# Softmax weights turned by VectorE's 32x32 block transposes and one trip through DRAM, from the tenth pair of heads on

## The chip, the core and the metric

The kernel runs on one core of one Trainium2 chip. The metric is the device time of one execution in microseconds (us). A core has five engines that run side by side, each through its own list of instructions in order: TensorE (PE in the profile; its weight loads are PEld), VectorE (DVE), ScalarE (ACT), GpSimd (POOL) and SyncE (SP). In this kernel SP issues every DMA; the DMAs run on 16 DMA engines and read or write DRAM.

## The reference

What is computed is windowed attention with a linear position bias, followed by two gated feed-forward blocks. Shapes: 4 sequences of 576 tokens (2304 rows), 8 heads of 64; the first block is 512 to 2048 and back, the second 512 to 1536 and back.

```python
def _attn_ref(q, k, v):
    scores = scale * np.matmul(q, k.transpose(0, 1, 3, 2))
    rel = pos[:, None] - pos[None, :]
    mask = (rel >= 0) & (rel < 128)
    scores = np.where(mask, scores + slopes * (-np.abs(rel)), -1e9)
    attn = softmax(scores)                       # over keys
    return np.matmul(attn, v)

def reference(q, k, v, w_in, w_out, w_gate, w_val, w_out2, rms_g):
    x = heads_side_by_side(_attn_ref(q, k, v))   # 2304 x 512
    h = x @ w_in
    x = (h * np.clip(h + 3, 0, 6) / 6) @ w_out
    xn = x / rms(x) * rms_g
    g = xn @ w_gate
    return (g * sigmoid(g) * (xn @ w_val)) @ w_out2
```

## The kernel before

**Blocks, pairs, steps.** The 2304 tokens are 18 tiles of 128 rows, taken as six blocks of three tiles. Attention works on a pair of heads at a time: four pairs for each block, 24 pairs in all, numbered 0 to 23. A pair has three steps, one for each tile of queries. Each query sees 128 keys, which lie in two neighbouring tiles, so a row of the upper key tile and a row of the lower one never both hold a live weight in the same column. From pair 9 on (`JOINT = 9`, the tenth) a step folds both key tiles into one 128x128 tile per head before the exponential (line 378) and unfolds them after the transpose with two `affine_select`s on POOL (line 407), one that keeps one side of the diagonal and one that keeps the other.

**One step.** `scores` (TensorE) makes queries times keys; `bias` (VectorE, lines 371 and 378) adds the bias; `exp` (ScalarE, line 386) takes the exponential and its sum, and POOL the reciprocal (lines 388 and 389); `divide` (VectorE, line 394) scales the rows. The weights then stand with queries on the partitions, while the product with V needs keys there. `transpose` turns them: one TensorE transpose for each head and live key tile, into PSUM (line 400). `weights` copies the result to an SBUF tile `pt` (ScalarE, line 405) and runs the two selects (POOL, line 407). `values` multiplies with V (TensorE, line 418).

**Slots.** The first feed-forward block runs in 96 slots, 16 for each block of tokens. A slot m holds a product with `w_in` into the PSUM tile `ps_h` (line 484, 12 matmuls), the gate on ScalarE and VectorE (lines 722, 723, 728, 734), which makes `g`, and the product of the slot before with `w_out` (line 497, 9 matmuls), which reads that slot's `g`. The attention of the next block of tokens is laid into the slots. For a pair whose first slot is t0 a table `plan` gives the slots of its parts (`S` scores, `D` divide, `T` and `L` transpose, `V` values), and a loop over the slots issues them at fixed places:

```python
t0, plan = AHEAD + M1 * (b - 1) - 2 + 4 * j, {"S": (0, 0, 0), "D": (1, 1, 2),
    "T": (None, 2, 3), "L": (1, None, None), "V": (5, 5, 5)}
```

Three numbers are the slots, after t0, of a pair's three steps. Pairs start four slots apart, so slots t0+4 and t0+5 of a pair are t0 and t0+1 of the next. `T` puts the transposes behind the slot's product with `w_in`, `L` behind the product with `w_out`. Nothing reorders instructions: each engine works in the order in which the code issues them.

**Other work in the slots.** From the third block on (called part 3 in the code) each slot but those with m % 4 = 2 also prepares a piece of the second block's weights: `W2.turn` converts one 512 KB piece on ScalarE and VectorE (lines 131 to 147), and SP loads a later piece (`load`, line 202) and stores the converted one (lines 224 and 230). There are 36 pieces. `Norm` scales the rows of the first block's result, turns them on TensorE (line 550) and stores them (`store`, line 541, the transfers `x<-yt`) in some of the slots. After the 96 slots comes the second feed-forward block (lines 845, 892), which the change does not touch.

## Time and profile before

| What | us |
|---|---|
| time, median of 3 runs (956.23 to 956.37) | 956.29 |
| span of the profiled execution, first to last instruction | 954.2 |
| TensorE matmuls busy in that span | 937.7 |
| VectorE busy | 640.5 |
| ScalarE busy | 454.2 |
| GpSimd busy | 186.3 |

The span is counted on the chip from the first to the last instruction; the 2.1 us by which the median is longer lie around it. The page gives the profiled execution's time by this span. Pairs 9 to 23 lie between about 140 and 460 us of it. A matmul's end is modelled and overlaps the start of the next, so what a matmul takes of TensorE's time is read from start to start.

### The profile page before, as it was taken

To read this page: it belongs to the slowest core of one execution; us is meant where nothing else is said; L and a number is where in the kernel's file an instruction comes from. 1 tells how busy PE (TensorE), PEld (TensorE's weight loads), DVE (VectorE), ACT (ScalarE), POOL (GpSimd) and SP (SyncE) were. 2 spreads that over 40 slices of the span, in tenths; PEclk is the share of its full clock that TensorE was granted. 3 is DMA by queue.
4 is the path that set the end of the run, shared out by engine and by line. 5 is a ranking of instruction groups with operands and counts; after the bars stand their busy time and mean duration, and the time that the engine had idled before them with its cause. 6 is when DMAs were issued, how large, how long until landed. Compare 5 with 4: busy or idle time off the path is not lost.

```text
span 954.2 us, 14654 instructions
## 1 busy us (share of the span) xinstructions
PE 937.7 (98%) x5336; PEld 832.9 (87%) x5336; DVE 640.5 (67%) x1336; ACT 454.2 (48%) x969; POOL 186.3 (20%) x327
## 2 busy tenths in 40 slices
PE   7899999999999999999999999999999999999998
PEld 4587888888888888888899999999999999999996
DVE  5788667555878777877467657777545577545555
ACT  6899566455666655655455453433131323231120
POOL 4333012332223332422124223310000000000000
PEclk8999999999999999999999999999999999999999
DMA  6555401113666555554355757866757555755521
GB/s 231 183 194 194 187 20 51 32 53 117 198 211 203 172 164 174 164 169 130 122 182 210 287 206 293 320 229 234 249 212 281 214 202 199 265 206 211 214 86 67
DMA packets 67432, 175.02 MB, mean 183 GB/s; under 512 B 5024, under 2 KB 41888, under 8 KB 62624
## 3 DMA queue, kind: packets, MB, share of 16 engines
q1 hardware_dynamic: 67360, 174.09, 52.2%
q8 instruction: 42, 0.69, 0.3%
q14 instruction: 30, 0.25, 0.1%
HBM read 130.03 MB, written 44.04 MB: 182 GB/s over the span
## 4 chain that ended last, share of the span: by engine, by line
PE 87%; DVE 6%; ACT 4%; issue 2%; POOL 1%; ACTq 0%; POOLq 0%; DVEq 0%
PE ps_o L497 19%; PE ps_h L484 18%; PE ps_y L892 15%; PE ps_o L845 10%; PE ps_S L845 8%; PE ps_A L845 6%; PE ps_h L845 4%; PE ps_av L418 2%; PE ps_t L400 2%; PE ps_s L357 1%; DVE wx L143 1%; PE ps_s L348 1%; ACT t L386 1%; ACT wx L136 1%; DVE t L371 1%
## 5 line engine op out<-in xcount | busy, mean ns | idle before, releaser
L497 PE MATMUL ps_o<-w,g 128*128 128x512 f32 x864 | 224.0, 402 | 2.1 <-DVE w L147 1.9
L484 PE MATMUL ps_h<-xs,w 128*128 128x384 f32 x1152 | 220.2, 339 | 0.0
L484 PEld LDWEIGHTS ps_h<-xs,w 128*128 128x128 f32 x1152 | 202.4, 188 | 5.8 <-issue 0.2
L497 PEld LDWEIGHTS ps_o<-w,g 128*128 128x128 f32 x864 | 156.2, 188 | 41.1 <-issue 6.3
L892 PE MATMUL ps_y<-wo,g 128*128 128x512 f32 x648 | 150.2, 390 | 0.5 <-DVE g L881 0.5
L892 PEld LDWEIGHTS ps_y<-wo,g 128*128 128x128 f32 x648 | 121.3, 188 | 25.1 <-DVE g L881 0.9
L723 DVE SCALAR_TENSOR_TENSOR t<-t,ps_h 128x384 f32<-128x384 f32 x96 | 53.2, 554 | 98.7 <-ACT t L722 98.6
L722 ACT ACTIVATE t<-ps_h,three 128x384 f32<-128x384 f32 x96 | 55.5, 578 | 84.1 <-PE ps_h L484 80.2
L899 DVE TENSOR_TENSOR y<-y,ps_y 128x512 f32<-128x512 f32 x90 | 61.7, 686 | 35.3 <-PE ps_y L892 35.0
L386 ACT ACTIVATE t<-t,m 128x128 f32<-128x128 f32 (+1 forms) x144 | 61.4, 428 | 29.4 <-DVE t L378 14.2
L728 ACT CAST g<-t 128x384 fp32r<-128x384 f32 x96 | 49.5, 516 | 47.5 <-DVE t L723 46.2
L734 DVE TENSOR_TENSOR g<-t,g 128x384 fp32r<-128x384 f32 x96 | 54.4, 567 | 23.3 <-ACT g L728 23.0
L868 ACT ACTIVATE r<-r 128x384 f32<-128x384 f32 x36 | 19.0, 527 | 105.6 <-DVE r L867 105.6
L845 PE MATMUL ps_o<-S,tw 128*128 128x384 f32 x336 | 66.2, 339 | 0.3 <-DVE t L865 0.3
L388 POOL TENSOR_SCALAR r<-den 128x2 f32<-128x2 f32 x72 | 27.4, 380 | 187.6 <-ACT t L386 186.0
L845 PEld LDWEIGHTS ps_o<-S,tw 128*128 128x128 f32 x336 | 59.3, 188 | 1.4 <-DVE u L856 0.8
L389 POOL TENSOR_TENSOR r<-r,minus 128x2 f32<-128x2 f32 x72 | 56.0, 778 | 6.0
L407 POOL TENSOR_SCALAR_AFFINE_SELECT pt<-pt 128x256 f32<-128x256 f32 x82 | 34.5, 421 | 107.5 <-ACT pt L405 104.5
L853 ACT COPY s<-ps_S 128x384 f32<-128x384 f32 x18 | 8.7, 481 | 86.9 <-PE ps_S L845 86.9
L371 DVE CUSTOM_DVE_ANT_0 t<-ps_s,rel 128x256 f32<-128x256 f32 (+2 forms) x128 | 45.2, 395 | 3.6 <-PE ps_s L357 3.6
L143 DVE SCALAR_TENSOR_TENSOR wx<-wx,wy 128x512 uint32<-128x512 uint32 (+1 forms) x52 | 44.2, 850 | 0.0
L136 ACT ACTIVATE wx<-wraw 128x512 f32<-128x512 f32 (+1 forms) x52 | 42.8, 824 | 0.0
(138 smaller groups left out, 1471.9 us busy)
## 6 DMA issues: line engine op xcount, KB each, us to landing
tw<-t SPq DMA_DIRECT2D x52, 896.0 KB, 6.3
wraw<-w SPq DMA_DIRECT2D x36, 512.0 KB, 4.1
wo<-w SPq DMA_DIRECT2D x18, 1024.0 KB, 4.9
wraw<-w SPq DMA_DIRECT2D x16, 1024.0 KB, 9.1
t<-th SPq DMA_DIRECT2D x12, 896.0 KB, 4.3
t<-tl SPq DMA_DIRECT2D x12, 896.0 KB, 4.3
b<-wx SPq DMA_DIRECT2D x24, 256.0 KB, 2.6
w<-w SPq DMA_DIRECT2D x12, 512.0 KB, 3.0
```

The source lines that it names most:

```text
L143: vec.scalar_tensor_tensor(out=xi, in0=xi, scalar=3, in1=y, op0=ALU.logical_shift_left, op1=ALU.bitwise_or)
L371: vec.tensor_tensor_reduce(out=self.t[:, a, c0:], in0=s[:, c0:], in1=(rel_split if self.i in SPLITS else rel)[:, c0:], scale=2.0 ** (-8.0 ...
L386: act.activation(p, p, AF.Exp, bias=self.m[:, a : a + 1], scale=-1.0, accum_out=self.den[:, a : a + 1])
L389: pool.tensor_tensor(self.r, self.r, minus, ALU.pow)
L484: pe.matmul(ps[:, : n * P], lhsT=w[:, a, c * P : (c + 1) * P], rhs=xs[c][:, b, : n * P], start=(k == 0), stop=(k == 3 * KC - 1),)
L497: pe.matmul(o, lhsT=g[:, a, i * P : (i + 1) * P], rhs=w[:, b], start=(m == first and a == 0 and b == 0), stop=(m == last and a == 1),)
L722: act.activation(r[:, :nq], ps[:, :nq], AF.Relu, bias=three)
L723: vec.scalar_tensor_tensor(out=r[:, :nq], in0=r[:, :nq], scalar=6.0, in1=ps[:, :nq], op0=ALU.min, op1=ALU.mult)
L734: vec.tensor_sub(g[:, 1, :nq], r[:, :nq], f32(g[:, 0, :nq]))
L845: pe.matmul(ps, lhsT=w[a][:, k, c * P : (c + 1) * P], rhs=x[:, b, c], start=(start and j == 0), stop=(j == 5), skip_group_check=True,)
L892: pe.matmul(ps, lhsT=gs[i + k][:, a, t // 3, t % 3 * P : (t % 3 + 1) * P], rhs=wo[i + k][:, b], start=(k == 0 and a == 0 and b == 0), stop ...
L899: vec.tensor_add(acc[t], acc[t], ps)
```

## The change

From pair 9 on a step's weights are no longer turned by TensorE. `turn` lets VectorE transpose the 32x32 blocks of each head's folded 128x128 tile in place of the grid (block row and block column stay where they are), from the upper half of the tile `t` into its lower half, and SP stores that half to a DRAM tile `pd` (128 KB, rows of 512 bytes). When a pair's three steps are stored, `fetch` reads them back with four DMAs, one for each group of 32 partitions, which put block (b, a) where block (a, b) was: 96 KB each, in runs of 32 elements (128 bytes). The result is the turned tile, in `pt`. The copy by ScalarE is gone, and the two selects on POOL stand in a method of their own. `pt` is one fixed tile with a place for each of the three steps, and its two middle dimensions are exchanged. In the slots, divide and values keep their places; `turn` stands in the slots of the divide, behind the low half of `g`; `fetch` (`R`) at the start of slot t0+3; the selects (`W`) of all three steps at the start of slot t0+4. Pairs 0 to 8 keep TensorE's transposes.

A second edit: the load of a later piece in `W2` moves from `turn` to the end of `begin`, so that it stands behind the first three conversion steps of the piece whose buffer it takes, and a piece is loaded one turn earlier than before.

```diff
@@ Second.begin and Second.turn
                 for _ in range(3):
                     next(self.run)
+                self.load()
...
             x = run.send(None)
-            self.load()
             if kind < 2:
                 self.begin()
                 sp.dma_start(out=self.whole[m][:, kind::2], in_=x.rearrange("p (a k) -> p a k", a=2))
@@ Pair
+        def fetch(self):
+            for k in range(0, P, 32):
+                sp.dma_start(
+                    out=weights_[k : k + 32, 1].rearrange("r u a (b s) -> r (u a b) s", s=32),
+                    in_=self.d[:, :, :, k : k + 32].rearrange("u a (b r) s -> r (u a b) s", r=32),
+                )
@@ Step
+            self.via = self.joint or self.c0 == P and pair.b * H // 2 + pair.j >= JOINT
+            self.pt = weights_[:, :, u]
...
+        def turn(self):
+            t, pr = self.t[:, :, :P], self.pair
+            if self.first:
+                pr.d = dram.tile([3, 2, P, P], F32, tag="pd", name="pd", bufs=2)
+            vec.transpose(t, self.t[:, :, P:])
+            sp.dma_start(out=pr.d[self.u].rearrange("a p k -> p a k"), in_=t)
...
         def weights(self):
-            self.pt = ap.tile([P, 2, 2, P], F32, tag="pt", name="pt", bufs=3)
-            act.copy(self.pt[:, :, self.p0 // P :], self.ps[:, :, self.p0 // P :])
+            act.copy(self.pt[:, self.p0 // P :], self.ps[:, self.p0 // P :])
+            self.select()
+
+        def select(self):
             for c, sign in ((0, -1), (1, 1)) if self.joint else ():
@@ the plan of a pair's steps
-            for kind, at in plan.items():
+            steps = {"S": plan["S"], "D": plan["D"], "R": (None, None, 3), "W": (4, 4, 4), "V": plan["V"]} if step.via else plan
+            for kind, at in steps.items():
@@ the loop over the slots
             late = l_
+            for x in r_:
+                x.pair.fetch()
+            for x in w_:
+                x.select()
             ps = ps_h.tile([P, 4 * P], F32, tag="h", name="ps_h")
...
             vec.tensor_sub(g[:, 1, :nq], r[:, :nq], f32(g[:, 0, :nq]))
+            for x in d_:
+                if x.via:
+                    x.turn()
```

Three places show what the order of instructions becomes. On TensorE, the five products after the values of pair 20 (`ps_av`), in which pair 21's three steps were turned (`ps_t`); `ps_h` and `ps_o` are the two products of a slot. Line 484 becomes 506, 497 becomes 519, 418 becomes 439.

```order
L418 MATMUL ps_av<-pt,vraw 64x128 x12
L497 MATMUL ps_o<-w,g 128x512 x9
L400 MATMUL ps_t<-ident,t 128x128 x2
L484 MATMUL ps_h<-xs,w 128x384 x12
L400 MATMUL ps_t<-ident,t 128x128 x2
L497 MATMUL ps_o<-w,g 128x512 x9
L484 MATMUL ps_h<-xs,w 128x384 x12
L400 MATMUL ps_t<-ident,t 128x128 x2
L497 MATMUL ps_o<-w,g 128x512 x9
```

```order
L439 MATMUL ps_av<-pt,vraw 64x128 x12
L519 MATMUL ps_o<-w,g 128x512 x9
L506 MATMUL ps_h<-xs,w 128x384 x12
L519 MATMUL ps_o<-w,g 128x512 x9
L506 MATMUL ps_h<-xs,w 128x384 x12
L519 MATMUL ps_o<-w,g 128x512 x9
```

The three groups of two transposes are gone, and nothing takes their place on TensorE.

On SP, slots t0+1 to t0+3 of pair 21 (`wraw` is the load of a piece of weights, `b` and `w` its converted store, `x<-yt` the store of a normed tile, `pd` and `pt` the new trip):

```order
L297 DMA vraw<-v 128x4x128
L202 DMA wraw<-w 128x512
L230 DMA w_4_133<-w 128x1024
L202 DMA wraw<-w 128x512
L224 DMA b_114<-wx 256x1x256
L541 DMA x_1_139<-yt 512x1x128
L202 DMA wraw<-w 128x512
L224 DMA b_114<-wx 256x1x256
```

```order
L298 DMA vraw<-v 128x4x128
L413 DMA pd<-t 128x2x128 x2
L202 DMA wraw<-w 128x512
L230 DMA w_4_133<-w 128x1024
L413 DMA pd<-t 128x2x128
L202 DMA wraw<-w 128x512
L224 DMA b_114<-wx 256x1x256
L563 DMA x_1_140<-yt 512x1x128
L323 DMA pt<-pd 32x24x32 x4
L202 DMA wraw<-w 128x512
L224 DMA b_114<-wx 256x1x256
```

The last of the three stores and the four reads stand with a load, a store of weights and a store of `x` between them.

On VectorE, slots t0+1 and t0+2 of a pair, after: the transposes stand behind the low half of `g` (line 760) and ahead of the scaling of the norm and the conversion of weights. Before, the same rows stood there without line 412.

```order
L760 TENSOR_TENSOR g<-t,g 128x384
L412 STREAM_TRANSPOSE t<-t 128x2x128 x2
L556 TENSOR_SCALAR y<-y,ri 128x512
L143 SCALAR_TENSOR_TENSOR wx<-wx,wy 128x512
L133 TENSOR_SCALAR wy<-wraw 128x512
L140 TENSOR_SCALAR wy<-wraw 128x512
L147 TENSOR_TENSOR w<-wx,w 128x512
L749 SCALAR_TENSOR_TENSOR t<-t,ps_h 128x384
L405 TENSOR_SCALAR t<-t,r 128x128 x2
L760 TENSOR_TENSOR g<-t,g 128x384
L412 STREAM_TRANSPOSE t<-t 128x2x128
```

Two steps of the pair are turned in slot t0+1 and the third in slot t0+2, where its divide (line 405, 394 before) is.

## Rows read from the trace of the kernel before

**Rows 1.** The page: span, and busy us with shares of the engines.

```profile
span 954.2 us, 14654 instructions
...
PE 937.7 (98%) x5336; PEld 832.9 (87%) x5336; DVE 640.5 (67%) x1336; ACT 454.2 (48%) x969; POOL 186.3 (20%) x327
```

**Rows 2.** Busy us (and instructions) by stretch: PE, PEld, DVE, ACT, POOL; clock, DMA share, GB/s.

```profile
300.00:400.00 100.00, 100.00 (x654) 87.90 (x653) 77.95 (x212) 61.15 (x161) 31.96 (x67) 1.00 0.53 168
```

**Rows 3.** Timeline of PE around pair 23: start us, us, what, count.

```profile
441.27 2.34 PE L497 MATMUL ps_o<-w,g 128*128 128x512 f32 x9
443.45 0.38 PE L400 MATMUL ps_t<-ident,t 128*128 128x128 f32 x2
443.58 2.34 PE L484 MATMUL ps_h<-xs,w 128*128 128x384 f32 x12
...
452.44 2.27 PE L484 MATMUL ps_h<-xs,w 128*128 128x384 f32 x12
...
460.29 2.33 PE L497 MATMUL ps_o<-w,g 128*128 128x512 f32 x9
462.46 2.27 PE L484 MATMUL ps_h<-xs,w 128*128 128x384 f32 x12
464.57 2.24 PE L497 MATMUL ps_o<-w,g 128*128 128x512 f32 x9
466.65 0.69 PE L484 MATMUL ps_h<-xs,w 128*128 128x384 f32 x3
```

**Rows 4.** Groups by line, 140 to 460 us: busy us, mean ns, idle before.

```profile
L407 POOL TENSOR_SCALAR_AFFINE_SELECT pt<-pt 128x256 f32<-128x256 f32 x82 | 34.5, 421 | 107.5 <-ACT pt L405 104.5
...
L400 PE MATMUL ps_t<-ident,t 128*128 128x128 f32 x90 | 17.4, 274 | 0.3 <-ACT pt L405 0.2
...
L405 ACT COPY pt<-ps_t 128x256 f32<-128x256 f32 x45 | 16.5, 366 | 3.9 <-PE ps_t L400 3.8
L378 DVE TENSOR_TENSOR t<-t 128x256 f32<-128x256 f32 x37 | 15.7, 425 | 1.3
```

**Rows 5.** Timeline of DVE, slot t0+2 of pair 21.

```profile
403.85 0.56 DVE L723 SCALAR_TENSOR_TENSOR t<-t,ps_h 128x384 f32<-128x384 f32 x1 [0.71 <-ACT t L722]
...
404.99 0.56 DVE L734 TENSOR_TENSOR g<-t,g 128x384 fp32r<-128x384 f32 x1 [0.16 <-ACT g L728]
...
407.04 0.46 DVE L140 TENSOR_SCALAR wy<-wraw 128x512 uint16<-128x512 uint16 x1
```

**Rows 6.** The page's DMA issues: count, KB each, median us to landing.

```profile
x<-yt SPq DMA_DIRECT2D x18, 256.0 KB, 3.0
```

**Rows 7.** Timeline of SP, pair 21: start and us of each issue.

```profile
407.19 0.57 SPq L541 DMA_DIRECT2D x<-yt  x1
407.87 0.58 SPq L202 DMA_DIRECT2D wraw<-w  x1
```

**Rows 8.** Timeline of SP, 143 to 150 us, where few transfers run.

```profile
149.01 0.38 SPq L297 DMA_DIRECT2D vraw<-v  x1
```

**Rows 9.** Stretches of 1 us, columns as in Rows 2: DMA share and GB/s.

```profile
112.00:113.00 1.00, 1.00 (x8) 1.00 (x7) 0.00 (x0) 0.00 (x0) 0.00 (x0) 1.00 1.00 426
144.00:145.00 1.00, 1.00 (x6) 0.81 (x5) 0.97 (x5) 0.89 (x4) 0.00 (x0) 1.00 0.77 199
145.00:146.00 1.00, 1.00 (x7) 0.95 (x6) 1.00 (x5) 0.77 (x4) 0.86 (x2) 1.00 0.72 260
...
150.00:151.00 1.00, 1.00 (x6) 0.83 (x5) 1.00 (x3) 1.00 (x2) 0.00 (x0) 1.00 0.49 144
151.00:152.00 1.00, 1.00 (x9) 0.92 (x6) 1.00 (x2) 1.00 (x2) 0.00 (x0) 1.00 0.42 126
```

**Rows 10.** Timeline of PE: the values of pair 21, slot t0+5.

```profile
418.18 1.53 PE L418 MATMUL ps_av<-pt,vraw 128*64 128x128 f32 x24
```

**Rows 11.** Timeline of POOL, slot t0+4 of pair 21: the next pair's reciprocals.

```profile
415.98 0.22 POOL L388 TENSOR_SCALAR r<-den 128x2 f32<-128x2 f32 x1 [5.92 <-ACT t L386]
416.28 0.87 POOL L389 TENSOR_TENSOR r<-r,minus 128x2 f32<-128x2 f32 x1
```

More of the change, by code (lines that the diff above doesn't have):

```diff
@@ L62 @@
 PAIRS2 = NTILE // 6
-KINDS = "QSDTLV"
+KINDS = "QSDTLVRW"
 OPEN = {"reuse_waits": "tile"}
@@ L274, in fused_kernel @@
     xs_of = {}
+    weights_ = ap.tile([P, 2, 3, 2, P], F32, tag="pt", name="pt", bufs=1)
     class Pair:
@@ L399, in transpose @@
                 for c in range(self.p0 // P, 2):
-                    pe.transpose(self.ps[:, a, c], self.t[:, a, c * P : (c + 1) * P], ident)
+                    pe.transpose(self.ps[:, c, a], self.t[:, a, c * P : (c + 1) * P], ident)
         def weights(self):
-            self.pt = ap.tile([P, 2, 2, P], F32, tag="pt", name="pt", bufs=3)
-            act.copy(self.pt[:, :, self.p0 // P :], self.ps[:, :, self.p0 // P :])
+            act.copy(self.pt[:, self.p0 // P :], self.ps[:, self.p0 // P :])
+            self.select()
+        def select(self):
             for c, sign in ((0, -1), (1, 1)) if self.joint else ():
                 pool.affine_select(
-                    out=self.pt[:, :, c], in_=self.pt[:, :, 1], compare_op=ALU.is_ge, fill=0.0,
+                    out=self.pt[:, c], in_=self.pt[:, 1], compare_op=ALU.is_ge, fill=0.0,
                     base=c - 1, pattern=[[0, 2], [sign, P]], channel_multiplier=-sign,
@@ L420, in values @@
                         lhsT=pr.vr[:, self.i - 1 + c - pr.lo, a * D : (a + 1) * D],
-                        rhs=self.pt[:, a, c],
+                        rhs=self.pt[:, c, a],
                         start=(c == self.from_),
@@ L577, in fused_kernel @@
     for t in range(AHEAD):
-        q, s_, d_, t_, _, v_ = at(t)
+        q, s_, d_, t_, _, v_, _, _ = at(t)
         scores(s_, t % 2)
@@ L699, in fused_kernel @@
             t, slot = slot, slot + 1
-            q, s_, d_, t_, l_, v_ = at(t)
+            q, s_, d_, t_, l_, v_, r_, w_ = at(t)
             go = p < 3 or last or (t - AHEAD) % 4 in (0, 3)
```

## The prediction

> **What bounds the kernel now.** Read the page's busy line first: TensorE's matmuls cover 98% of the 954.2 us, VectorE comes next with 67% [rows 1]. Then the stretch that holds the changed pairs: from 300 to 400 us TensorE is busy for all 100.00 us at clock 1.00 (the level of 2.4 GHz), VectorE for 77.95, ScalarE for 61.15, GpSimd for 31.96, and the DMA engines for 0.53 of it [rows 2]. So there TensorE is the bound and waits for nobody: an instruction taken from it shortens the time by what it holds of the array, an instruction given to another engine costs nothing until TensorE waits for it, and a new wait of TensorE costs its full length. The profiled span is 954.2 us against a median of 956.29; I add the 2.1 us around the span back by working on 956.3.
>
> **Removed: 90 transposes and 45 copies.** The 90 transposes have a mean of 274 ns and a busy time of 17.4 us [rows 4], but both overlap with neighbours; what counts is from start to start. In pair 23, from the product at 441.27 to the one at 452.44, three products with w_out, two with w_in and three groups of two transposes take 11.17 us [rows 3]. Without transposes the same products take: the first, behind the values, 462.46 - 460.29 = 2.17; a product with w_in 464.57 - 462.46 = 2.11; one with w_out 466.65 - 464.57 = 2.08. So 2.17 + 2 x 2.11 + 2 x 2.08 = 10.55, and the pair's transposes hold 0.62 us. A group's own step is only 443.58 - 443.45 = 0.13; the rest is the slower change-over around it. From 0.13 x 3 x 15 = 5.9 us to 0.62 x 15 = 9.3 us; I take 9.3, since it is measured over the whole sequence. The 45 copies at 366 ns [rows 4] leave ScalarE, which nobody on the path waits for there: 0.
>
> The Trainium skill ("TensorE: Matmul & The Clock Gate", Part 4: PE-mode transpose) gives about 275 ns for a 128x128 transpose inside a kernel. The mean agrees with it, but the chain of starts does not charge it; 90 times that would be 24.7 us and a time of 931.6, the last rival below.
>
> **Added on VectorE: 45 block transposes of 128x256.** The trace has none. The nearest row is the fold of the same 128x256 values, 425 ns [rows 4]. Lower bound 0 (they might vanish in idle time), upper bound twice the fold, 0.85 us, if the blocks go through twice. I take 0.43: 45 x 0.43 = 19 us over some 310 us, which lifts VectorE from 78% to about 84%. In slot t0+1 two of them stand ahead of the weight conversion and of line 723 of the next slot, which had idled 0.71 us before it started at 403.85 [rows 5]: 0.86 - 0.71 = 0.15 us later. TensorE needs the product tile only behind its next product, some 2 us on. Cost 0; at the upper bound line 723 is 1.0 us late, still inside those 2 us.
>
> **Added: the trip through DRAM, whose length decides.** Take pair 21, one of those with the most traffic around it. Its third step is the last. VectorE finishes the low half of g at 404.99 + 0.56 = 405.6 [rows 5]; the block transpose ends at 406.0. The store is issued then: 128 KB, against 3.0 us to landing for a store of 256 KB in runs of the same 512 bytes [rows 6], so it lands by 409. In SP's order a load of weights, a store of weights and a store of x come before the reads. The moved load waits for line 140, which ends at 407.50, or at 407.9 with the transpose ahead of it [rows 5]. Each issue takes up to 0.6 us [rows 7]: the three end at 409.7, after the landing, so the store's landing hardly delays this pair. The four reads are issued from 409.7 to 412.
>
> They also stand behind 512 + 256 + 256 KB in the DMA engines. A lone load issued at 149.01 [rows 8] moves its data in the stretches from 150 to 152 [rows 9], over 1 us after its issue, so the load of 407.9 moves from 409.1. At 426 GB/s [rows 9] its 512 KB take 1.25 us; the weights' store, 256 runs of 1024 bytes, takes 0.86 and the store of x, 512 runs of 512 bytes, 0.9 by the prices worked out next (54 and 28 ns a run): the reads' data start at about 412.1.
>
> The four reads make 3072 runs of 128 bytes, 192 on each of 16 engines. Nothing in the trace moves such runs. The lone load has 512 runs of 512 bytes and 0.49 + 0.42 = 0.91 us of all engines: 0.91 x 16 / 512 = 28 ns a run. The load of keys and queries between 144 and 146 has 256 runs of 1792 bytes on average and 1.49 us: 93 ns a run. The line through both falls to 9 ns at 128 bytes. So 9 to 28 ns if a run never costs more when it is shorter; above 28 nothing in the trace sets an end. I take 15, near the line, since the cost fell in proportion between the two rows. That is 2.9 us (1.7 to 5.4), landing at 415.0 (413.8 to 417.5).
>
> When must they have landed? The values of pair 21 start at 418.18 [rows 10], 0.2 earlier without the transposes between, and take 1.5 us for three steps; the third step starts at 419.0. POOL runs six selects ahead, at 0.42 us [rows 4] and a little between, 2.7 us in all; five must be done by then, the sixth 0.2 us later. The reads must land by 419.2 - 2.7 - 0.1 = 416.4. At 15 ns 1.4 us are left; at 28 ns TensorE waits 1.1 us. POOL also has the next pair's reciprocals behind the waiting selects: the first began at 415.98 and its power takes 0.87 [rows 11]. They would end 1 to 1.5 us late, and VectorE's divide behind them delays that slot's g by as much; TensorE reads it almost one slot, some 4 us, later. Cost 0.
>
> Other pairs have more room. Six of the twelve pairs that lie beside the weight traffic (12 to 23) have such a store of x ahead of the reads, as the order of SP shows; without it the reads go 0.6 to 0.9 us earlier. Pairs 9 to 11 have no weight traffic and some 4 us to spare. The moved load gives a piece one turn more to arrive, and the reads add 2.9 us and the stores 3 x 256 x 28 / 16 ns = 1.3 us of DMA time to a pair's 21 us: the share goes from 0.53 to 0.73. Cost 0.
>
> **Sum.** 956.3 - 9.3 + 0 = 947.0.
>
> **The rivals.**
>
> *The reads land late and give it back.* At 28 ns six pairs wait 1.1 us and six some 0.4: 6.6 + 2.4 = 9.0 us, so 956.0. At 20 to 28 ns part of the gain goes: 948 to 956. For it speaks that SP, the DMA engines and POOL all take this trip in order.
>
> *Slower: the runs of 128 bytes cost more than those of 512.* The place is the four reads, the consequence TensorE waiting in line 418 for the selects. It decides from about 28 ns: above it each nanosecond costs 0.19 us in each of 12 pairs, 2.3 us in all. At 33 ns 968, at 40 ns 984. For it: each run is a separate read of DRAM with a row step of 512 bytes. Against: up to now fewer bytes meant less time.
>
> The Trainium skill ("DMA: Bandwidth & Descriptors", Specifications) asks for at least 512 bytes a transfer for full rate, which speaks against this change but names no price; by it this rival would be the forecast, and no row of before shows it.
>
> *Far slower: the strided reads run at a small part of the full rate.* If a run of 128 bytes cost as much as the dearest of the rows, 93 ns, a pair's reads would take 17.9 us in place of 2.9: landing at 430.0, a wait of 13.6 us in twelve pairs and some 9.6 in pairs 9 to 11, 192 us, a time near 1139. Against it: those 93 ns moved 14 times the bytes.
>
> The Trainium skill ("VectorE: DVE Perf Modes", The three transpose paths) warns that a plain DMA copy which transposes by strides is 19 times slower than the hardware's own; a nineteenth of 426 GB/s would be 17.5 us for the 384 KB of a pair, about the same. Here the strides move blocks and a run stays 128 bytes long, and nothing run so far shows the like.
>
> *The transposes were worth their whole mean.* 931.6, from 274 ns. The starts speak against it.
>
> **How the numbers follow.** The trip stays hidden (time 945 to 949): 0.56. Late and given back in part or whole (949 to 958): 0.18. Slower by runs over 28 ns: 0.22. Far slower: 0.02. Whole mean saved: 0.02. About 0.2% (1.9 us) is what a measurement of this kernel can tell from no change. Faster by more than that: 0.56 + 0.02 and a good third of 0.18 (949 to 954.4), with the rest of it at no change or just above: faster 0.65, same 0.09, slower 0.26. The range begins at 945, 2 us under the sum for the gain that a removed group's neighbours may add, and reaches 968, where the runs cost 33 ns; I leave about 0.15 above it and 0.03 below.
>
> **What would show it.** Right: no line 400 after pair 8; products of about 2.1 us follow each other with nothing between; line 418 (439 now) starts with no idle time; the reads land before the slot t0+5 of their pair, some 3 us after their last issue. Wrong: TensorE or its weight loads idle before the values, released by POOL's selects, and these by the DMA `pt<-pd`; DMA stretches behind the reads that are full at few GB/s; or VectorE so late that the product with w_in waits for line 723.

## The result, and the profile after

The changed kernel takes 967.53 us (median of 4 runs, 966.92 to 968.59) against 956.26 before (955.97 to 956.37): 1.0118 of the time before, 95% interval 1.0105 to 1.013. It is 11.3 us slower, where 947.0 was forecast. The span of the profiled execution is 966.2 us.

The page of the kernel after, in the form of [rows 1], and the stretch from 300 to 400 us, in the form of [rows 2]:

```profile
span 966.2 us, 14705 instructions
...
PE 939.9 (97%) x5246; PEld 824.6 (85%) x5246; DVE 656.5 (68%) x1381; ACT 439.5 (45%) x924; POOL 183.6 (19%) x327
```

```profile
300.00:400.00 100.00, 95.49 (x579) 79.06 (x578) 77.38 (x207) 53.39 (x132) 26.12 (x56) 1.00 0.73 198
```

TensorE, which had been busy for all 100.00 us, now idles in 4.5 of them, though it has less to do. The DMA share is 0.73, as forecast. What the engines wait for between 130 and 480 us (engine, tile and line that wait, what released them: us, times, longest):

```profile
POOL pt L428 <- DMA pt<-pd: 158.8, 13, 17.0
...
DVE t L405 <- POOL r L400: 14.1, 15, 2.1
PEld ps_h L506 <- DVE t L749: 13.8, 15, 2.4
...
ACT yt L561 <- DMA x<-yt: 11.1, 3, 4.0
PEld ps_av L439 <- POOL pt L428: 10.9, 37, 1.1
PE ps_h L506 <- DVE t L749: 8.3, 13, 2.0
```

Two families stand there. The first starts at the reads `pt<-pd`: POOL's selects wait for them, the values (`ps_av`) wait for the selects, and VectorE's divide (line 405) waits for POOL's reciprocals. The second starts at the store `x<-yt`: ScalarE's copy waits for the one `yt` buffer. Both can delay line 749 on VectorE, which releases the product tile for TensorE (`ps_h`); the first also holds TensorE directly, at the values.

Pair 21 shows the first family. The timelines of VectorE, SP, POOL, TensorE and VectorE again, around the pair's trip (start us, us, what; idle before it):

```profile
414.69 0.44 DVE L412 STREAM_TRANSPOSE t<-t 128x256 f32<-128x256 f32 x1
```

```profile
415.16 0.37 SPq L413 DMA_DIRECT2D pd<-t  x1
417.13 0.33 SPq L202 DMA_DIRECT2D wraw<-w  x1
417.51 0.52 SPq L224 DMA_DIRECT2D b<-wx  x1
418.12 0.57 SPq L563 DMA_DIRECT2D x<-yt  x1
418.86 4.89 SPq L323 DMA_DIRECT2D pt<-pd  x4
```

```profile
426.16 2.54 POOL L428 TENSOR_SCALAR_AFFINE_SELECT pt<-pt 128x256 f32<-128x256 f32 x6 [10.26 <-DMA pt<-pd]
428.79 0.22 POOL L399 TENSOR_SCALAR r<-den 128x2 f32<-128x2 f32 x1
```

```profile
426.62 2.58 PE L439 MATMUL ps_av<-pt,vraw 128*64 128x128 f32 x24 [0.73 <-POOL pt L428]
429.13 2.34 PE L519 MATMUL ps_o<-w,g 128*128 128x512 f32 x9
```

```profile
429.83 0.48 DVE L405 TENSOR_SCALAR t<-t,r 128x128 f32<-128x128 f32 x2 [2.09 <-POOL r L400]
```

The turn ends at 414.69 + 0.44 = 415.13. The reads are issued 3.7 us later, as forecast, but the four issues take 4.89 us and the selects find their data at 426.16, 11.0 us after the turn; the forecast's deadline was 10.4. The values start 0.73 us late and take 2.58 us in place of 1.53 [rows 10]. The next pair's first reciprocal starts at 428.79, behind the selects, and the divide behind it had waited 2.09 us.

### The profile page after: what moved, and what is told of

Same layout as the page of the kernel before. It is cut to its first block, busy times and chain, and to the rows that moved or that the text cites. A ratio compares the mean times of both kernels' runs of the same rounds, so it can differ in the third digit from the quotient of the medians.

```text
span 966.2 us, 14705 instructions
## 1 busy us (share of the span) xinstructions
PE 939.9 (97%) x5246; PEld 824.6 (85%) x5246; DVE 656.5 (68%) x1381; ACT 439.5 (45%) x924; POOL 183.6 (19%) x327
## 4 chain that ended last, share of the span: by engine, by line
PE 70%; DVE 10%; ACT 6%; DMA 5%; issue 4%; POOL 4%; SPq 2%; POOLq 0%; ACTq 0%; DVEq 0%
PE ps_y L921 15%; PE ps_h L506 12%; PE ps_o L519 11%; PE ps_o L874 10%; PE ps_S L874 7%; PE ps_A L874 6%; PE ps_h L874 4%; DMA pt<-pd 2%; SPq L323 2%; PE ps_av L439 2%; ACT wx L136 2%; DVE wx L143 2%; POOL pt L428 2%; DMA x<-yt 2%; POOL r L400 1%
## 5 line engine op out<-in xcount | busy, mean ns | idle before, releaser
L428 POOL TENSOR_SCALAR_AFFINE_SELECT pt<-pt 128x256 f32<-128x256 f32 x82 | 36.5, 460 | 177.1 <-DMA pt<-pd 158.8
L400 POOL TENSOR_TENSOR r<-r,minus 128x2 f32<-128x2 f32 x72 | 53.9, 749 | 6.0
L405 DVE TENSOR_SCALAR t<-t,r 128x128 f32<-128x128 f32 (+1 forms) x144 | 36.8, 303 | 19.1 <-POOL r L400 18.8
L439 PE MATMUL ps_av<-pt,vraw 128*64 128x128 f32 x544 | 46.2, 294 | 2.9 <-POOL pt L428 1.8
```

What stands on the lines that cost most here:

```text
L400: pool.tensor_tensor(self.r, self.r, minus, ALU.pow)
L428: pool.affine_select(out=self.pt[:, c], in_=self.pt[:, 1], compare_op=ALU.is_ge, fill=0.0, base=c - 1, pattern=[[0, 2], [sign, P]], channe ...
L439: pe.matmul(pr.acc[a * D : (a + 1) * D, self.u], lhsT=pr.vr[:, self.i - 1 + c - pr.lo, a * D : (a + 1) * D], rhs=self.pt[:, c, a], start=( ...
```

## The experiments

All times are medians; the ratio is to the kernel before on the same chip, with its 95% interval.

| Run | What is different | us | ratio |
|---|---|---|---|
| x7_no_trip_load_back | after, no trip, load in old place | 950.28 | 0.9939 (0.9924 to 0.9954) |
| x2_no_trip | after, no trip | 956.85 | 1.0011 (1.0002 to 1.0021) |
| x5_before_moved_load | before, load moved | 957.63 | 1.0015 (1.0005 to 1.0024) |
| x6_after_load_back | after, load in old place | 956.38 | 1.0008 (0.9999 to 1.0018) |
| x3_no_selects | after, no selects | 955.03 | 0.9987 (0.9978 to 0.9997) |
| x1_fetch_early | after, reads behind the last store | 960.02 | 1.0039 (1.0026 to 1.0052) |
| x4_runs_512 | after, reads in runs of 512 bytes | 963.04 | 1.0069 (1.0054 to 1.0084) |
| x8_two_x_buffers | after, two `yt` buffers | 964.59 | 1.0093 (1.0078 to 1.0108) |
| x10_selects_behind | after, selects behind the reciprocals | 1003.44 | 1.0494 (1.0478 to 1.051) |
| x9_early_fetch_load_back | x1 and x6 together | 992.59 | 1.0385 (1.0367 to 1.0402) |
| x11_early_back_behind | x9 and x10 together | 1038.65 | 1.0871 (1.085 to 1.0891) |
| x12_early_back_loads_act | x9, loads issued by ScalarE | 959.77 | 1.0035 (1.0023 to 1.0048) |
| x13_back_loads_act | x6, loads issued by ScalarE | 963.02 | 1.0078 (1.006 to 1.0096) |
| x14_slot_later_load_back | x6, trip one slot longer | 958.93 | 1.0027 (1.0018 to 1.0037) |
| x15_slot_later | after, trip one slot longer | 966.40 | 1.0117 (1.0099 to 1.0136) |
| x16_quiet_pairs | x6, trip in pairs 9 to 11 alone | 954.30 | 0.998 (0.9971 to 0.9989) |

### The parts one by one

**x2**: the trip is left out, the block transposes and the moved load stay.

```diff
-            sp.dma_start(out=pr.d[self.u].rearrange("a p k -> p a k"), in_=t)
...
-            for x in r_:
-                x.pair.fetch()
```

> Leaves out the trip: no stores of turned tiles and no reads; the block transposes on VectorE stay, and the selects and values work on what an earlier pair left in the tile. Shows what the removed transposes are worth alone. If the prediction's term of 9.3 us holds: 947. If the block transposes cost something on VectorE, or the gain was smaller: 948 to 953. If VectorE is the new bound by itself: near 967, as with the trip.

956.85 lies between the last two of these, so none of the three holds as it stands.

**x7**: the same, with the load of weights back in its old place.

```diff
                 for _ in range(3):
                     next(self.run)
-                self.load()
...
             x = run.send(None)
+            self.load()
```

> As x2 (leaves out the stores of turned tiles and the reads, so the values work on what an earlier pair left), with the load in its old place. Theory C: what kept x2 at 956.8 was the moved load: 947 to 950, and the prediction's 9.3 us for the transposes stand. Theory D (the block transposes on VectorE themselves cost what the removed ones gave): 954 to 957, with TensorE waiting for VectorE's line 744.

950.28, just above theory C's range, against 956.85: without any trip the moved load alone costs 6.6 us. SP's timeline at the same turn of x7 (first) and x2 (second) shows how:

```profile
332.52 0.45 SPq L202 DMA_DIRECT2D wraw<-w  x1
337.97 0.33 SPq L230 DMA_DIRECT2D w<-w  x1
338.40 0.53 SPq L560 DMA_DIRECT2D x<-yt  x1
```

```profile
338.21 0.33 SPq L202 DMA_DIRECT2D wraw<-w  x1
338.66 0.35 SPq L230 DMA_DIRECT2D w<-w  x1
339.12 0.53 SPq L560 DMA_DIRECT2D x<-yt  x1
```

The rows come in the same order. But in the old place the load's buffer has been free since the turn before, so it goes out 5.45 us ahead of the weights' store; moved, it waits for this turn's conversion (line 140), and the store, which stands behind it on SP, goes out 0.45 us after it, the store of x right behind. Between 215 and 455 us the median distance from a load to the store of weights behind it is 3.4 us (`b`) and 5.3 us (`w`) in x7, 0.4 us for both in x2. DMA issues between 215 and 455 us, x7 first, then x2 (count, KB each, median us to landing):

```profile
b<-wx SPq DMA_DIRECT2D x24, 256.0 KB, 2.5
w<-w SPq DMA_DIRECT2D x11, 512.0 KB, 2.9
x<-yt SPq DMA_DIRECT2D x10, 256.0 KB, 3.1
```

```profile
b<-wx SPq DMA_DIRECT2D x24, 256.0 KB, 4.3
w<-w SPq DMA_DIRECT2D x11, 512.0 KB, 5.0
x<-yt SPq DMA_DIRECT2D x10, 256.0 KB, 4.4
```

The same bytes land 1.3 to 2.1 us later. The timelines of ScalarE, VectorE and TensorE of x2 show what the store of 339.12 holds up, and the last row the stretch of the third such place:

```profile
344.59 0.59 ACT L558 COPY yt<-ps_x 128x512 f32<-128x512 f32 x1 [3.73 <-DMA x<-yt]
```

```profile
345.69 0.55 DVE L744 SCALAR_TENSOR_TENSOR t<-t,ps_h 128x384 f32<-128x384 f32 x1 [2.92 <-ACT t L743]
```

```profile
346.30 1.49 PE L503 MATMUL ps_h<-xs,w 128*128 128x384 f32 x7 [2.05 <-DVE t L744]
```

```profile
430.00:435.00 5.00, 4.64 (x24) 4.25 (x26) 3.60 (x8) 2.71 (x5) 0.00 (x0) 0.66 0.41 138
```

ScalarE stands 3.73 us at the copy, the gate behind it on ScalarE is late, and TensorE waits 2.05 us. This comes three times (at 262, 346 and 430 us). After the last, the granted clock averages 0.66 over 5 us, with TensorE busy for 3.39 of the 5 us before: between the levels of 1.2 and 2.4 GHz that is 3.4 us at the lower one, 1.7 us lost. After the other two it stayed at 1.00. From 130 to 480 us TensorE idles 6.1 us in x2 and 1.1 in x7; with the 1.7 us that makes up the 6.6.

**x5**: the kernel before with the load moved, and nothing else.

```diff
                 for _ in range(3):
                     next(self.run)
+                self.load()
...
             x = run.send(None)
-            self.load()
```

> The kernel before with the second edit alone: the load of a later piece of weights behind the conversion steps of the same turn, so that it goes out directly ahead of the weights' store and the store of x. Theory C (this bunching delays the store of x, whose single buffer ScalarE then waits for): the landing of the weights' store goes from 2.6 us to some 4.3 as without the trip, ScalarE waits some 4 us more for x, but here TensorE runs about 4 us later at that place, since its transposes are still there, so the time moves little: 956 to 958. If the moved load is harmless: 956 and landings near 2.6.

957.63: here it costs 1.5 us, as theory C had it. The stores land as late as in x2 (4.3, 5.2 and 4.4 us) and ScalarE's copy waits 9.4 us in three places, but TensorE hardly waits. The same delay costs 6.6 us in x2, where the transposes are gone from TensorE and the block transposes have come to VectorE; which of the two makes the difference was not separated.

**x6**: the change with the load in its old place; the diff is that of x7.

> The changed kernel with the load back in its old place (issued as soon as the slot's turn begins, one turn later than the changed one). Theory C: the weights' and x's stores land near 3 us again, ScalarE's 11.1 us of waits for x shrink to about 3, the reads of pt are issued about 1.5 us earlier: 955 to 961. If C is wrong: 966 to 968. Against: the load then stands behind SP's wait for the store of a turned tile and may come late for its conversion; then 965 or more with VectorE or ScalarE waiting for wraw.

956.38, in theory C's range: against x7 the trip costs 6.1 us, against the changed kernel the move costs 11.1. Moved load and trip together cost 17.2 us over x7, 4.6 more than their two prices. Beside the weight traffic the reads now reach the selects 7.9 to 9.5 us after the last store's issue; but the loads of slot t0+3 stand behind the reads in SP's order, and ScalarE waits for pieces of weights (11.8 us in 11 places; before, 1.2 us in one).

### The reads, POOL and the runs

**x3**: the changed kernel without the masks of pairs 9 to 23; the trip and the moved load stay.

```diff
-            for x in w_:
-                x.select()
```

> Leaves out the selects (masks) from pair 9 on, so POOL's reciprocals wait for nothing and the values wait for the reads alone. If most of the loss comes through POOL's order (reciprocals behind the selects, and 2.7 us of selects behind the landing): VectorE's 18.8 us of waits for POOL go and the time is 947 to 951. If it is the landing itself that TensorE waits for: 957 to 964.

955.03, between its two expectations and below x2, which has no trip at all. So what the trip costs in the changed kernel, 967.5 - 956.9 = 10.7 us, reaches TensorE by way of the selects: without them the same stores and reads cost it nothing. The selects need the data 2.7 us before the values do, and they stand ahead of the reciprocals on POOL; x3 takes away both at once. TensorE's starts divide them. The values of pair 21 in x2, whose selects wait for no read:

```profile
414.99 1.53 PE L436 MATMUL ps_av<-pt,vraw 128*64 128x128 f32 x24
416.45 2.34 PE L516 MATMUL ps_o<-w,g 128*128 128x512 f32 x9
```

From the values' start to the next product's these are 1.46 us, against 429.13 - 426.62 = 2.51 in the changed kernel. Over pairs 8 to 23 the steps add up to 22.5 us in x2, 22.6 in x3 and 30.1 in the changed kernel. So 7.6 of the 10.7 us are values that run at the pace of the late selects. About 3 are left for the reciprocals and for TensorE's wait ahead of the values (0.73 us in pair 21); no run separates these two.

**x1**: the reads right behind the last store, in slot t0+2.

```diff
                     x.turn()
+                    if x.last:
+                        x.pair.fetch()
```

> The four reads of a pair stand right behind its last store, ahead of the weight load, weight store and x store of that slot and the next. Theory A (the reads are late because they are issued and moved behind about 1 MB of other transfers): landing falls from 11 us after the last block transpose to about 6.5, the waits of TensorE before the values and of VectorE for the reciprocals vanish, and the time is 946 to 950. Theory B (runs of 128 bytes are slow in themselves, wherever they stand): the landing moves by the 3.7 us of issue at most and 961 to 966 is left. A price of A: SP stands still for the store's landing, some 2 us, ahead of the weight load; if that load comes late, 950 to 956.

960.02, between its theories: the four issues take 2.03 us each time, and the values' steps are back at 22.6 us; three stalls behind the store of x remain. In this profile the granted clock fell after each of them, 5.1 us lost in all against 1.7 in x2. These 3.4 us are most of the 4.8 by which the two profiled executions differ, so little is left for the reads themselves.

**x4**: the reads in runs of 512 bytes, so that the blocks are not exchanged.

```diff
-                    out=weights_[k : k + 32, 1].rearrange("r u a (b s) -> r (u a b) s", s=32),
-                    in_=self.d[:, :, :, k : k + 32].rearrange("u a (b r) s -> r (u a b) s", r=32),
+                    out=weights_[k : k + 32, 1].rearrange("r u a s -> r (u a) s"),
+                    in_=self.d[:, :, k : k + 32].rearrange("u a r s -> r (u a) s"),
```

> The four reads move the same bytes to the same partitions in runs of 512 bytes on both sides; the blocks are then not exchanged. 768 runs for 3072. Theory B: near 947. Theory A: the reads' own 2.5 us become about 1.3, they are still issued behind the other transfers, and half or more of the loss stays: 955 to 963.

963.04, at the upper edge of theory A: 4.5 us come back of the 10.7 that the trip costs beside the moved load, and the values' steps fall to 25.8 us. Short runs carry less than half of the trip's price, and the 6.6 us of the move are not theirs. What a run costs can be read in the changed kernel at a pair with nothing beside it, the reads issued at 159.14 (columns as in [rows 9]):

```profile
160.00:161.00 1.00, 1.00 (x6) 0.91 (x6) 0.83 (x2) 1.00 (x3) 0.00 (x0) 1.00 0.84 134
161.00:162.00 1.00, 1.00 (x7) 1.00 (x7) 0.94 (x2) 1.00 (x2) 0.00 (x0) 1.00 0.95 150
162.00:163.00 1.00, 1.00 (x8) 0.73 (x8) 1.00 (x2) 1.00 (x2) 0.00 (x0) 1.00 0.70 109
```

(0.84 + 0.95 + 0.70) x 16 / 3072 = 13 ns a run, against 28 for one of 512 bytes: the forecast had taken 15.

**x8**: two `yt` buffers while the weights are prepared.

```diff
-                junk = ypool.tile([P, DM], F32, tag="yt", name="junk", bufs=1)
+                junk = ypool.tile([P, DM], F32, tag="yt", name="junk", bufs=1 + (self.b < 4))
...
-                yt = ypool.tile([P, KC, P], F32, tag="yt", name="yt", bufs=1)
+                yt = ypool.tile([P, KC, P], F32, tag="yt", name="yt", bufs=1 + (self.b < 4))
```

> The changed kernel with two buffers for the normed tile that waits to be stored (one before), so ScalarE does not wait for the store of x to land. Theory C: 11.1 us of ScalarE's waits and the three long waits of TensorE for line 749 with the slow clock behind them vanish: 958 to 963. If these waits are harmless: 966 to 968.

964.59, between the two expectations: the copy waits no more, 2.9 us come back. The divide then waits 20.0 us for the reciprocals in place of 14.1: when one family is cured, the other takes part of the gain.

**x10**: the selects at the end of slot t0+4, behind the next pair's reciprocals.

```diff
-            for x in w_:
-                x.select()
...
             for x in s_:
                 x.exp()
+            for x in w_:
+                x.select()
```

> The changed kernel, with the six selects on POOL of a pair moved from the start of slot t0+4 to its end, behind the reciprocals of the next pair. Everything else as changed, the load included. Theory A (selects that wait for the reads hold the reciprocals, the reciprocals VectorE's divide, the divide the next slot's gate and that TensorE): the waits of line 405 for the reciprocals fall from 19 us to under 3 and the waits of TensorE for the gate's tile from 8.3 to 4 or 5 us; the values still wait, 10 us or somewhat more, since the selects start no earlier. Time 961 to 964. Rival B (the reciprocals are a symptom; what holds TensorE is the ScalarE copy behind the x store and the late reads alone): 966 to 968.

1003.44: both expectations missed. The third reciprocal waits for the last exponential of the slot, so the selects came later than the reads would have let them, and the values waited for them (28.4 us on TensorE, up to 2.7 at once). Another 17.0 us went to the granted clock, which lay under 1.00 in 16 stretches of 5 us between 170 and 490 us. The divide's waits are gone, but the slots are so much longer that the run can't price the reciprocals.

### Whose place on SP

**x9**: the early reads of x1 with the load in its old place.

> The changed kernel with both cures at once: the load of the weights back in its old place and the four reads issued directly behind the pair's last store, in slot t0+2, not at the start of t0+3. Theory A (the loss is made of three things: the stores and the x copy held up by the moved load, the reads issued too late, POOL's order behind them): nothing of the trip is left on TensorE's path, so the time comes near the version without any trip, 950.3 us; I expect 951 to 953, with POOL's waits for the reads under 5 us and TensorE's waits for VectorE under 2 us. Rival B (the trip costs by its mere DMA traffic, wherever it is issued): it stays at 955 to 957, as in the version with the load alone put back (956.4).

992.59, 40 us above theory A and worse than x1 and x6 alone. SP, VectorE and TensorE of x9 at one pair:

```profile
260.67 0.36 SPq L413 DMA_DIRECT2D pd<-t  x1
264.01 2.04 SPq L323 DMA_DIRECT2D pt<-pd  x4
266.10 0.71 SPq L202 DMA_DIRECT2D wraw<-w  x1
```

```profile
271.11 0.43 DVE L133 TENSOR_SCALAR wy<-wraw 128x512 uint32<-128x512 uint32 x1 [2.86 <-DMA wraw<-w]
```

```profile
273.12 2.18 PE L506 MATMUL ps_h<-xs,w 128*128 128x384 f32 x11 [1.85 <-DVE t L747]
```

SP stands at the reads until 264.01, for the landing of the store of 260.67, and the next load goes out at 266.10. VectorE waits 2.86 us for its piece, the gate's instructions stand behind the conversion, and TensorE waits. In x1 the moved load had one turn more to arrive and did not feel this: the move, which costs 6.6 us, also protects. Part of the loss is clock. Two stretches of x9, in the form of [rows 2]:

```profile
390.00:395.00 5.00, 2.47 (x13) 1.97 (x12) 2.91 (x11) 1.93 (x4) 1.71 (x5) 0.98 0.86 320
395.00:400.00 5.00, 4.63 (x34) 3.85 (x33) 3.47 (x14) 3.37 (x15) 3.25 (x6) 0.68 0.00 1
```

TensorE was busy for 2.47 of 5 us, and over the next 5 the clock averaged 0.68. Nine such stretches between 345 and 495 us lie under 1.00 and lose 8.5 us.

**x12** and **x13**: in x9 and x6 the loads of weights are issued by ScalarE, in a queue of their own.

```diff
-                sp.dma_start(out=raw, in_=w2[i // 3, :, (i % 3) * DM : (i % 3 + 1) * DM])
+                act.dma_start(out=raw, in_=w2[i // 3, :, (i % 3) * DM : (i % 3 + 1) * DM])
```

> Load back in its old place and reads issued directly behind the pair's last store (the version that took 992.6 us), and the loads of the weights' pieces issued by ScalarE in place of SP, at the same place of a slot. Theory A (the 36 us of that version are loads that stand in SP's order behind reads which wait there 3 us for the landing of the last store and take 2 us more to issue): the conversion finds its piece, TensorE's waits for the gate fall from 27 us to under 3, the selects find their data; time 951 to 956. Rival B (the DMA engines are what is short, the order of issues only shows it): no better than 980, with the pieces landing as late as before.

> Load back in its old place, reads at the start of slot t0+3 as in the change (the version that took 956.4 us), and the loads of the weights' pieces issued by ScalarE in place of SP. Theory A (of the 6.1 us which the trip costs there, most comes from the loads that stand behind the four reads in SP's order): ScalarE's waits for the pieces, 11.8 us in that version, go, and the time falls to 952 to 954. Rival B (the rest is late reads and DMA traffic): 956 again, within 1 us.

x12 comes down by 33 us to 959.77, above theory A's range but far below B's: most of x9's loss came from the order on SP. But x13 rises, from 956.38 to 963.02, against both of its theories. Its waits from 200 to 460 us:

```profile
DVE t L405 <- POOL r L400: 17.8, 19, 1.7
PEld ps_av L439 <- POOL pt L428: 12.3, 43, 0.8
```

ScalarE's waits for pieces are gone (0.9 us), but the loads now run beside the reads, which land after 5.2 us (median) in place of 3.9, and the first family is back.

**x11**: x9 with the selects behind the reciprocals.

> Load back in its old place, reads issued behind the last store, and the selects behind the next pair's reciprocals. Theory A: with the reads early the selects find their data, so POOL's order no longer matters: the same as the version with the load back and the early reads, within 1 us (951 to 953). Rival B (selects behind the reciprocals end later and now hold the values): 2 us or more above it.

1038.65, 82.6 us over before: nearly the losses of x9 and x10, 36.5 and 47.4, added up. Of these 27.3 us are granted clock under 1.00. Theory A missed, since x9 and x10 had.

### More time for the trip, and a quiet place for it

**x14** (load in its old place) and **x15** (moved): reads, selects and values one slot later for three of four pairs.

```diff
-            steps = {"S": plan["S"], "D": plan["D"], "R": (None, None, 3), "W": (4, 4, 4), "V": plan["V"]} if step.via else plan
+            z = j < 3
+            steps = {"S": plan["S"], "D": plan["D"], "R": (None, None, 3 + z), "W": (4 + z,) * 3, "V": (5 + z,) * 3} if step.via else plan
```

> Load back in its old place, and for the first three pairs of a block the reads, the selects and the values each one slot later (reads at the start of slot t0+4, selects of t0+5, values in t0+6); the fourth pair of a block, whose values are due in the block's last slot, as in the change. Slot t0+4 has no weight turn, so no load stands behind those reads in the same slot. Theory A (what the trip costs with the load put back, 956.4 against 950.3 us, is the time it has: reads too late for the selects and loads too late for the conversion): three quarters of the 6.1 us come back, 951 to 953, ScalarE's waits for the pieces 11.8 us fall to 3 to 5, VectorE's divide waits for nothing. Rival B (the cost is the traffic on the DMA engines, whenever it runs): 955 to 957.

> The changed kernel with the moved load as it is, and for the first three pairs of a block the reads, the selects and the values each one slot later. Theory A (the moved load costs by the late reads and by the stores that it holds up): the reads are in time for nine of twelve pairs, VectorE's waits for the reciprocals (14 us) fall to under 5 us; what is left is the three stalls behind the stores of x, as in the version without the trip (956.9): 957 to 960. Rival B: the moved load holds everything up by its traffic: 964 or more.

958.93 and 966.40: neither gains. x14 lies above both of its theories, x15 where theory B had it. In x14 the divide waits for nothing, but ScalarE's line 136 waits for the loads, which land after 4.7 us in place of 4.3 in x6:

```profile
ACT wx L136 <- DMA wraw<-w: 18.0, 15, 2.8
```

In x15 the divide's wait fell to 0.6 us as theory A had it, yet the values still waited for the selects (3.5 us on TensorE, 12.6 on its weight loads), which now stood behind the next pair's reciprocals, and the copy for the store of x waited 12.3 us. Giving the reads more time moved the wait to another transfer.

**x16**: the trip in pairs 9 to 11 alone, the load in its old place.

```diff
-            self.via = self.joint or self.c0 == P and pair.b * H // 2 + pair.j >= JOINT
+            self.via = (self.joint or self.c0 == P) and JOINT <= pair.b * H // 2 + pair.j < 12
```

> VectorE's block transposes and the trip only in pairs 9 to 11, which have no weight traffic beside them; pairs 12 to 23 keep TensorE's transposes, and the load stands in its old place. Theory A (a pair whose trip finds the DMA engines free gains the 0.62 us that its transposes hold, and pays nothing): 956.1 - 3 x 0.62 = 954.2, that is 0.998 of the time before, with no wait of TensorE for the gate or for the values in these pairs. Rival B (the trip costs a pair about 0.4 us wherever it is, as the 6.1 us over fifteen pairs would give on average): 956.1 - 3 x 0.2 = 955.5, not to be told from no change.

954.30, as theory A had it to 0.1 us, and faster than both kernels (0.998, interval 0.9971 to 0.9989). The values of pairs 8 to 11 on TensorE, first in x16, then the first and last of them before:

```profile
147.41 1.53 PE L439 MATMUL ps_av<-pt,vraw 128*64 128x128 f32 x24
...
167.49 1.53 PE L439 MATMUL ps_av<-pt,vraw 128*64 128x128 f32 x24
...
187.57 1.53 PE L439 MATMUL ps_av<-pt,vraw 128*64 128x128 f32 x24
...
207.83 1.53 PE L439 MATMUL ps_av<-pt,vraw 128*64 128x128 f32 x24
```

```profile
147.44 1.53 PE L418 MATMUL ps_av<-pt,vraw 128*64 128x128 f32 x24
```

```profile
209.84 1.53 PE L418 MATMUL ps_av<-pt,vraw 128*64 128x128 f32 x24
```

60.42 us in place of 62.40: three pairs gain 1.98, 0.66 each, and TensorE waits for neither the gate nor the selects.

## Why the prediction was wrong

From 956.1, the transposes off TensorE give -5.8 (x7), the moved load +6.6 (x2), the trip +10.7, all of it by way of the selects (x3): with rounding, 967.5. The order matters: with the load in its old place the trip costs 6.1 (x6). In the sum of the prediction these three stood at -9.3, 0 and 0. That 967.5 still lies in its range is luck: the upper end was there for runs at 33 ns, and they cost 13.

- **The transposes hold 0.62 us a pair: right.** x16 shows 0.66 a pair where nothing else is short. In x7, beside the weight traffic too, 5.8 of 9.3 us came. From values to values nine of its 15 steps are 0.58 to 0.71 us shorter than before; the other six, all beside the weight traffic, gain 0.8 us together. There TensorE's weight loads wait 4.5 us for line 744, the counterpart of 749. That fits the longer VectorE work; no run took it apart.
- **The block transpose at 0.43 us: right.** The row above has 0.44, the mean between 140 and 460 us is 427 ns. Whether its cost is 0 is not shown: it may be part of the 3.5 us that x7 misses.
- **"The moved load gives a piece one turn more to arrive ... Cost 0": the first step that failed.** The benefit was seen, and x9 shows that it is real. What was not priced is what the load now waits for: this turn's conversion, with the weights' store right behind it on SP. Two transfers that had gone out 3.4 to 5.3 us apart go out together, the stores land 1.3 to 2.1 us later, and one of them guards a single buffer. That costs 6.6 us without the trip and 11.1 with it. The order of rows on SP did not show it; the wait ahead of the load does.
- **The landing at +9.0: mis-sized, and the second step that failed.** The reads' issue at +3.7 us was right, the run was at 13 ns for 15, and the selects started 2.4 us after the last issue, where 3.0 was forecast. But four issues beside the weight traffic took 4.89 us, not 2.3, and the data came at +11.0. The deadline of +10.4 was too late as well: TensorE was ready for the values at 426.62 - 0.73 = 425.89, 10.8 us after the turn where the forecast had 12.0. By its own rule (the data 1.6 us ahead of the values) that makes +9.2. The 1.8 us between are what the values lost: 0.73 of wait and 1.05 of slower running. With 7.6 us over all pairs this is most of the trip's price, and the 28 ns that the rival wanted was not needed for it.
- **"POOL also has the next pair's reciprocals ... Cost 0": the third.** They ended late as written. By the prediction's own rows that was 415.0 + 2.7 - 415.98 = 1.7 us and not 1 to 1.5; at the divide it became 2.1. The slack of "almost one slot" was not there: TensorE waits for the product tile that line 749 releases, and the next slot's line 749 stands on VectorE behind that divide. Such waits of TensorE went from 5 (5.9 us) in x2 to 13 (8.3 us). Of the 10.7 us about 3 are left for them and for the wait ahead of the values.
- **The rivals.** "Slower by the price of runs" named the right sign and fell by its mechanism: 128 bytes cost 13 ns and not over 28, though runs of 512 bytes gave back 4.5 us (x4). "Late and given back" had the right mechanism in part, and its 956 is the time of x6, where the load is in its old place; with the move in, the same lateness goes below zero. "Far slower" fell with the 13 ns, and "the whole mean saved" with the 0.66 us a pair.

The Trainium skill ("DMA: Bandwidth & Descriptors", Specifications) asks for at least 512 bytes a transfer for full rate. The trace agrees that short runs lose rate (150 GB/s at a DMA share of 0.95, where the lone load in runs of 512 bytes had 144 at 0.49 [rows 9]), but x4, which keeps the rule, is still slower than before: the rule pointed the right way and not to the larger part of the cost. The Trainium skill ("VectorE: DVE Perf Modes", The three transpose paths) makes a plain copy that transposes by strides 19 times slower than the hardware's own where the innermost stride at the target is large. That slowness did not come, with runs of 128 bytes: a pair's reads took 2.5 us of all engines, where the estimate from that figure was 17.5.

Behind the failed steps is one view: costs were taken one by one against the slack that each had before. The slack was shared. Each repair of one wait (x8, x9, x13, x14) lengthened another. That stores, loads and reads share one order on SP and one set of DMA engines fits this; it is shown for the order by x12 against x9, and argued for the rest. Why four issues take 2.0 us alone and 4.9 beside other traffic is half settled. In x9 they took 2.02 to 2.04 us at each of pairs 9 to 22; x12 only puts the loads into ScalarE's queue, so that they run beside the reads, and eight of its pairs took 2.5 to 3.3. So traffic beside them stretches the issues; by what means no run shows.

## What to carry to other kernels

Here the removed transposes were worth their step where the transfer that replaced them had the DMA engines to itself (x16, 2 us gained in three pairs); over all fifteen pairs nothing was gained (x6). Look for the quiet places and take such a change there first. When a DMA is moved, ask what it waits for now and which transfers are released by the same event, since they will go out together. A slack may be spent once: before two edits are costed at nothing, see whether they spend the same one.

## What was unexpected of the hardware

- Four reads of 768 runs each took SP 2.04 us to issue at 159.14 and 4.89 at 418.86, beside the weights' load and stores.
- Runs of 128 bytes cost 13 ns against 28 ns for 512: the DMA engines moved 150 GB/s with them at a share of 0.95, where the kernel before reached 426 [rows 9].
- A store of 256 KB landed in 2.5 us when a 512 KB load had been issued 3.4 us ahead of it, and in 4.3 when it had been issued 0.4 us ahead (medians), at nearly the same DMA share (0.53 in x7, 0.56 in x2).
- A stall of TensorE of 2 us can have a price behind it: 0.66 mean granted clock over the next 5 us in x2. It came after one of three such stalls in x2, after all three in x1, and after none in the profile of the changed kernel. In x9, x10 and x11 the clock took 8.5, 17.0 and 27.3 us.
